# A Mamba-2 scan followed by a hardswish MLP: reordering the opening, and one weight load in four transfers

## The chip, the core and the metric

The kernel runs on one core of one Trainium2 chip. The core has five engines that run side by side, each through its own list of instructions in order: TensorE (PE; weight loads appear as PEld), VectorE (DVE), ScalarE (ACT), GpSimd (POOL) and SyncE (SP), which here only issues DMA transfers. They wait for each other through semaphores. Data come from HBM to the on-chip memory SBUF by DMA; TensorE writes to the eight banks of PSUM. The metric is the device time of one execution in microseconds (us).

## The reference

The first block is a chunked state-space scan over x (4 batches, 8 heads, 768 tokens, 32 channels) with decays a and matrices B and C (16 states). Per chunk it computes

```
cum = cumsum(log(clip(a)))                 # row sums of the logs, per head
L   = exp(cum_i - cum_j), lower triangle
y   = ((C B^T) * L) x  +  (C state) * exp(cum)
state = exp(cum_last) * state + sum_j B_j x_j exp(cum_last - cum_j)
```

The second block takes y as 3072 tokens of 256 features and computes `g = h * clip(h + 3, 0, 6) / 6` with `h = y @ w_in` (256 x 2048), and then `g @ w_out` (2048 x 256). The weights w_in and w_out are float64 in the input.

## The kernel before, in words

The tokens are cut into six chunks of 128 per batch, k = 0 to 5, each with all four batches (512 columns). For a chunk the scan gives yT (features by tokens); then the MLP runs over 16 tiles f of 128 hidden units. For chunk 0 the MLP's first product is `mlp_in` (L647), two full fp32 products for each f; later chunks split the operands (L715). `first_out` (L772) is chunk 0's second product. While the MLP of one chunk runs, the scan of the next is woven into it. The order on every engine is written out by hand in the body of the kernel: what the code calls first stands first in the engine's list, and there is no scheduler.

The float64 weights have to be turned into float32 on the chip. `load_w(i)` starts the DMA of one of eight parts of 1 MB (0 to 3 of w_in, 4 to 7 of w_out) into one of three buffers `raw`, and the generator `decode(i)`, advanced by `weights(i, n)` n steps at a time, does the arithmetic: copy out the top 16 bits (L198, ScalarE), build the significand (L201, L205, VectorE), mask out exponent and sign (L215, L217, VectorE), shift the exponent with two ScalarE activations (L221, L223), join exponent and sign (L228, VectorE) and multiply significand and power into the weight tile (L236, VectorE).

The opening, before the loop over chunks, prepares chunk 0. SyncE issues a, eight transfers of C, x, and the second part of the weights; ScalarE's queue issues the first part and B. The logs of a are summed by `add_up` in two stretches: tokens 0 to 255 first (needed at once for chunks 0 and 1), the other 512 later (L269). The second stretch is stored to DRAM by `store_rows` (L286 `cum_e`, L288 `cum_d`), and later chunks read it back as broadcasts. `turn_cum` (L316) transposes it on TensorE into c_ps, and `by_token` (L319) negates it into cum_n, which biases later chunks' exponentials (L385). For chunk 0, `diff` (L348, L357) makes the differences of sums in PSUM, `diff_exp` (L365) their exponentials L; `ends` (L396, GpSimd) scales B; `turn_b` (L422, L431) transposes B; `turn_squares` (L465) and `part_heads` (L475) transpose C and part it by heads once C has landed; `fade` (L481, GpSimd) scales it; `scores` (L530, and L548 for the state), `multiply` (L564, L574, L579), `mix` (L625, L503) and `keep` (L639) finish yT of chunk 0. `busy(n, bank)` (L493) issues n full-size products of the identity whose result nobody reads.

PSUM banks carry tags: f0 to f3 in one pool, o and y0, y1 in others; a tile with a tag waits until the readers of the tag's last tile are done.

## Time and profile before

| | us |
|---|---|
| median of 3 runs | 340.89 (340.2 to 341.09) |
| the profiled execution | 339.78 |
| its span, first to last instruction | 337.6 |
| TensorE busy | 330.6 (98%) |
| VectorE busy | 234.5 (69%) |
| ScalarE busy | 199.4 (59%) |
| GpSimd busy | 123.9 (37%) |
| first `mlp_in` product (L647) starts | 22.53 |

The profile is of one execution. Durations in it are those of single instructions; a busy share is an average over stages with different limits, and TensorE's busy time is modelled. Each idle time of an engine is put down to what ended it. The chain of waits goes back from the last instruction to whatever released it. L numbers are lines of the kernel before; in the changed kernel the same lines stand three to five further down.

### The profile page before, as it was taken

Reading aid. Unit: us, or ns where it says so; the run is one execution under the profiler, and the core shown is the slowest. Engines: PE = TensorE matmul, PEld = TensorE weight load, DVE = VectorE, ACT = ScalarE, POOL = GpSimd, SP = SyncE. Lnnn points to the kernel's source line nnn. Section 1 sums busy time; section 2 is a strip of 40 time slices with the busy share of each in tenths; the row PEclk is TensorE's granted clock in tenths of the full one; section 3 lists DMA queues with packets and bytes.
Section 4 is the critical chain, followed back from the end, with each engine's and each line's share of the span. In section 5 each row is a group of like instructions: output and inputs, shape, how many; then the busy total and the mean of one; then the engine's idle time right before and its main releaser. Section 6 shows DMA issues by size and latency. Waiting matters only on the chain.

```text
span 337.6 us, 8192 instructions
## 1 busy us (share of the span) xinstructions
PE 330.6 (98%) x3337; PEld 265.4 (79%) x3337; DVE 234.5 (69%) x380; ACT 199.4 (59%) x418; POOL 123.9 (37%) x123
## 2 busy tenths in 40 slices
PE   6999999999999999999999999999999999999996
PEld 2554448888888888888888888888888888899995
DVE  6699999998399739755339556355477355599974
ACT  4769878757986670576461576570486030577661
POOL 3300000290184799089813079911079800000000
PEclk9999999999999999999999999999999999999999
DMA  8999968042590215258107267101160001110001
GB/s 174 165 316 201 208 219 184 2 54 76 139 142 1 57 37 139 33 72 78 33 13 156 33 83 69 28 4 17 27 81 2 2 2 18 26 21 2 1 2 62
DMA packets 89605, 25.15 MB, mean 75 GB/s; under 512 B 82208, under 2 KB 85952, under 8 KB 89056
## 3 DMA queue, kind: packets, MB, share of 16 engines
q1 hardware_dynamic: 85184, 23.33, 37.5%
q10 hardware_dynamic: 4384, 1.31, 1.8%
q8 instruction: 26, 0.43, 0.5%
q14 instruction: 11, 0.09, 0.1%
HBM read 21.33 MB, written 3.29 MB: 73 GB/s over the span
## 4 chain that ended last, share of the span: by engine, by line
PE 94%; DMA 3%; DVE 1%; SPq 1%; issue 0%; DVEq 0%
PE h L715 33%; PE wb L914 13%; PE wc L914 8%; PE o L772 8%; PE h L647 8%; PE wa L914 8%; PE o_end L880 6%; PE y L625 3%; PE y L503 2%; PE cb L530 2%; DMA raw<-in_moe_w_in_dram 2%; DMA pairs<-in_C_dram 1%; PE y L548 1%; SPq L101 1%; PE o_end L898 1%; PE sp L548 0%
## 5 line engine op out<-in xcount | busy, mean ns | idle before, releaser
L759 DVE SCALAR_TENSOR_TENSOR gT<-gT,h 128x512 f32<-128x512 f32 x96 | 64.8, 684 | 33.8 <-ACT gT L754 32.2
L754 ACT ACTIVATE gT<-h,half 128x512 f32<-128x512 f32 x96 | 65.2, 685 | 25.6 <-PE h L715 23.6
L735 ACT ACTIVATE h<-h 128x512 f32<-128x512 f32 x66 | 38.2, 585 | 39.0 <-PE h L715 38.8
L715 PE MATMUL h<-y_hi,w_part 128*128 128x512 f32 x160 | 51.5, 407 | 0.0
L715 PE MATMUL h<-y_less,w_part 128*128 128x512 f32 x160 | 50.1, 399 | 0.0
L715 PE MATMUL h<-y_lo,w_part 128*128 128x512 f32 x160 | 49.5, 395 | 0.0
L818 POOL TENSOR_TENSOR s<-gT 128x512 f32<-128x512 f32 x16 | 23.8, 1490 | 46.7 <-DVE gT L759 46.7
L715 PEld LDWEIGHTS h<-y_lo,w_part 128*128 128x128 f32 x160 | 30.0, 188 | 7.3
L715 PEld LDWEIGHTS h<-y_hi,w_part 128*128 128x128 f32 x160 | 30.0, 188 | 6.8 <-DVE gT L759 0.2
L715 PEld LDWEIGHTS h<-y_less,w_part 128*128 128x128 f32 x160 | 29.2, 188 | 6.0 <-ACT h L735 0.2
L385 ACT ACTIVATE L<-L,cum_n 128x64 f32<-128x64 f32 x128 | 31.6, 336 | 0.0
L772 PE MATMUL o<-w_out,gT 128*128 128x256 f32 x128 | 28.8, 381 | 0.0
L647 PE MATMUL h<-yT,w_in 128*128 128x512 f32 x64 | 27.7, 594 | 0.0
L772 PEld LDWEIGHTS o<-w_out,gT 128*128 128x128 f32 x128 | 24.1, 190 | 3.8 <-issue 0.5
L647 PEld LDWEIGHTS h<-yT,w_in 128*128 128x128 f32 x64 | 12.1, 190 | 14.9 <-issue 13.2
L158 POOL TENSOR_SCALAR_AFFINE_SELECT L<-L 64x1024 f32<-64x1024 f32 (+1 forms) x16 | 20.4, 1281 | 8.5 <-DMA L<-cum_d 8.0
L579 DVE TENSOR_TENSOR L<-L,cb 128x512 f32<-128x512 f32 x24 | 15.0, 681 | 11.7 <-PE cb L530 11.7
L403 POOL TENSOR_TENSOR tmp<-state,eto 128x256 f32<-128x256 f32 x5 | 3.2, 643 | 52.8 <-ACT eto L389 48.9
L818 POOL TENSOR_TENSOR s<-gT,s 128x512 f32<-128x512 f32 x16 | 21.7, 1364 | 0.9
L396 POOL TENSOR_TENSOR bs<-B,L 128x128 f32<-128x128 f32 x24 | 11.2, 486 | 29.5 <-ACT L L385 20.9
L880 PE MATMUL o_end<-v_pair,g_pair 128*128 128x256 f32 x120 | 21.1, 281 | 0.0
L818 POOL TENSOR_TENSOR gT<-gT 128x512 f32<-128x512 f32 x16 | 20.4, 1279 | 0.9
(140 smaller groups left out, 593.0 us busy)
## 6 DMA issues: line engine op xcount, KB each, us to landing
raw<-in_moe_w_out_dram SPq DMA_DIRECT2D x4, 1024.0 KB
L<-cum_d SPq DMA_DIRECT2D x8, 512.0 KB
xt<-in_x_dram SPq DMA_DIRECT2D x6, 512.0 KB
raw<-in_moe_w_in_dram SPq DMA_DIRECT2D x3, 1024.0 KB
out_dram<-back SPq DMA_DIRECT2D x128, 16.0 KB
pairs<-in_C_dram SPq DMA_DIRECT2D x40, 32.0 KB
eto<-cum_e SPq DMA_DIRECT2D x20, 64.0 KB
B<-in_B_dram SPq DMA_DIRECT2D x5, 256.0 KB
```

The costliest lines, as they stand in the source:

```text
L158: nc.gpsimd.affine_select(out=t[rows], in_=t[rows], pattern=pattern, compare_op=ALU.is_ge, fill=-1e5, base=base, channel_multiplier=-1)
L385: nc.scalar.activation(Ls[c][:, b, h], Ls[c][:, b, h], AF.Exp, bias=cum_n[:, c, g:g + 1])
L579: nc.vector.tensor_tensor(out=Ls[c][:, :, hs], in0=Ls[c][:, :, hs], in1=cbs[c][q], op=ALU.mult)
L647: nc.tensor.matmul(out=h, lhsT=w_in[f // FP][:, j, f % FP * P:(f % FP + 1) * P], rhs=yTs[k][:, j].rearrange("p b i -> p (b i)"), start=(j ...
L715: nc.tensor.matmul(out=hs_[k, f], lhsT=w[j][:, f % FP * P:(f % FP + 1) * P], rhs=y[:, j], start=(start and j == 0), stop=True, skip_group_ ...
L735: nc.scalar.activation(h, h, AF.Copy, scale=1.0 / EPS + 1.0)
L754: nc.scalar.activation(gTs[k][:, f], h, AF.Relu, bias=half, scale=1.0 / 6.0)
L759: nc.vector.scalar_tensor_tensor(out=g, in0=g, scalar=1.0, in1=h, op0=ALU.min, op1=ALU.mult)
L772: nc.tensor.matmul(out=o[:, b % 2], lhsT=gTs[0][:, f, b * P:(b + 1) * P], rhs=w_out[:, f], start=(f == 0 and b % 2 == 0), stop=True, skip_ ...
L818: nc.gpsimd.tensor_tensor(out=o, in0=p_, in1=q_, op=op)
L880: nc.tensor.matmul(out=ends_["cross" if n == 2 else "squares"][b], lhsT=g_parts[t][n][:, b * P:(b + 1) * P], rhs=w, start=(t == 0 and b < ...
L914: nc.tensor.matmul(out=bank[:, slot], lhsT=lhs[:, j], rhs=rhs[:, j], start=(clear and j == 0), stop=True, skip_group_check=True)
```

## The change

It has five parts, all in the opening.

- The load of weight part 1 is split by columns into four transfers of 256 KB (rows of 1 KB instead of 4 KB).
- `add_up` of the second stretch is called before `ends(0, b)`, so on VectorE it stands before the transpose of C instead of behind `part_heads`.
- `turn_cum` and `by_token` follow `turn_b`, before the last two `diff`s of chunk 1; c_ps has bank f2 instead of f1, and cum_n is made by ScalarE instead of VectorE. One of the three `busy` products of the stretch, the one behind `turn_cum`, is dropped.
- One step of `decode(0)` (the first ScalarE activation, L221) is called before `turn_b`, so it stands before the copy of B's transpose on ScalarE.
- `decode(0)` has one more step: joining exponent and sign (L228) is now apart from the last product (L236). With the same later calls, it stands before the products of `multiply` (L579) on VectorE, where it had been behind them.

```diff
@@ load_w
-        queue.dma_start(out=dst, in_=src)
+        cuts = range(NP if i == 1 else 1)
+        for c in cuts:
+            sl = slice(c * src.shape[-1] // len(cuts), (c + 1) * src.shape[-1] // len(cuts))
+            queue.dma_start(out=dst[:, :, sl], in_=src[:, :, sl])
@@ decode
         nc.vector.tensor_tensor(out=e, in0=e, in1=s, op=ALU.bitwise_or)
+        if i == 0:
+            yield
         m, e = m.bitcast(FP32), e.bitcast(BF16)
@@ by_token
-        nc.vector.tensor_scalar(
-            out=cum_n[:, 2:], in0=c_ps[:, 2:], scalar1=-1.0, scalar2=None, op0=ALU.mult)
+        nc.scalar.mul(cum_n[:, 2:], c_ps[:, 2:], -1.0)
@@ the opening
     first_eto()
     diff(1, 2, 3)
     weights(0, 1)
+    add_up(ends_at[1])
     for b in range(NB):
         ends(0, b)
+    weights(0, 1)
     turn_b(0)
+    c_ps = ps.tile([P, NC, G], FP32, name="c_ps", tag="f2")
+    turn_cum(c_ps)
+    by_token(c_ps)
     diff(1, 0, 1)
     weights(0, 1)
     diff_exp(1, 2)
     diff_exp(1, 3)
     turn_squares(bcs[0][0], turned(0)[2])
     part_heads(0)
     fade(0, HALF[1], nc.gpsimd)
-    add_up(ends_at[1])
     store_rows()
     load_w(2)
     weights(0, 1)
     busy(2, ps.tile([P, NB * P], FP32, name="d", tag="f3"))
     scores(0)
     multiply(0)
     load_w(3)
-    c_ps = ps.tile([P, NC, G], FP32, name="c_ps", tag="f1")
-    turn_cum(c_ps)
-    busy(1, ps.tile([P, NB * P], FP32, name="d", tag="f0"))
     weights(0, 1)
     weights(1, 1)
-    by_token(c_ps)
     mix(0)
     keep(0)
     weights(1, 3)
```

## The prediction, made before the changed kernel ran

> **What bounds the kernel now.** I read the chain of waits first, because it says which work set the end. TensorE holds 94% of it; the DMA, VectorE and queue pieces all lie in the opening. In order of time, the chain between the last load of C and the first stage of the MLP is:

> ```profile
> 8.91 4.00 DMA pairs<-in_C_dram
> ...
> 13.09 1.17 DVE csT L465
> ...
> 14.28 0.89 DVE cT L475 x2
> ...
> 15.30 1.25 PE cb L530 x59
> ...
> 16.56 1.30 DVE L L579 x2
> ...
> 17.90 0.43 PE c_ps L316 x4
> 18.33 1.05 PE d L493 x2
> 19.39 1.00 PE y L625 x57
> 20.38 0.61 PE y L503 x16
> 20.99 1.00 PE y L625 x54
> 21.99 0.61 PE y L503 x16
> 22.60 27.66 PE h L647 x64
> ```

> Columns: start, length, piece, in us. From 22.5 us on there is nothing but TensorE: 64 matmuls of L647 in 27.66 us are 0.432 us each, without a gap, and the rest of the chain is TensorE until the last VectorE addition at 334.46. So a microsecond saved before the first L647 matmul is saved at the end, as long as TensorE's suppliers keep up. And two pieces of the chain, c_ps (L316) and d (L493, the matmul of `busy`), are not needed by the mix that follows them: they only stand ahead of it on TensorE.

> Second, the timeline of the two engines that feed this stretch, VectorE:

> ```profile
> 13.09 1.16 DVE L465 STREAM_TRANSPOSE csT<-pairs 128x512 f32<-128x512 f32 x1 [2.86 <-DMA pairs<-in_C_dram]
> 15.07 1.21 DVE L269 TENSOR_TENSOR_SCAN pre<-pre 32x512 f32<-32x512 f32 x1
> 16.56 2.48 DVE L579 TENSOR_TENSOR L<-L,cb 128x512 f32<-128x512 f32 x4 [0.28 <-PE cb L530]
> 18.95 0.68 DVE L228 TENSOR_TENSOR we<-we,ws 128x1024 uint16<-128x1024 uint16 x1
> 20.82 0.28 DVE L319 TENSOR_SCALAR cum_n<-c_ps 128x128 f32<-128x128 f32 x1
> ```

> and ScalarE:

> ```profile
> 11.95 0.59 ACT L431 COPY bT<-t_ps 128x512 f32<-128x512 f32 x1 [0.90 <-PE t_ps L422]
> 17.32 0.37 ACT L564 COPY adds<-y 128x256 f32<-128x256 f32 x1 [1.73 <-PE y L548]
> 18.75 1.15 ACT L198 COPY ws<-raw 128x1024 uint16<-128x1024 uint16 x1 [0.53 <-DMA raw<-in_moe_w_in_dram]
> ```

> What to see: VectorE idles 2.86 us before the transpose of C, and ScalarE 0.90 and 1.73 us; these are the holes into which the change moves work. The 0.53 us before L198 says that the second load of weights lands at about 18.75.

> **The change part by part.**

> *Row sums (L269) earlier.* On VectorE the scan goes from behind L475 to behind L217, which ends at 10.23. Its input (L266) has been there since 5.27. It takes 1.21 us, so it ends at 11.5, inside the 2.86 us hole: cost nothing. Without that cover it would cost 1.21.

> *c_ps and cum_n.* The four transposes of L316 go behind those of B (t_ps ends at 11.91; the scan is done by then). They take 0.36 to 0.43 us and push the difference matmuls and the two `busy` matmuls, which ended at 14.88, to 15.24 to 15.31. TensorE had 0.43 us idle before cb at 15.30, waiting for cT, so the delay of cb is 0 to 0.1; I take 0. cum_n becomes a ScalarE copy: no row has it, the nearest are L574 (128x128, 0.31 each of two) and L319 itself (0.28), so 0.3. ScalarE now runs L221 in the hole before bT, then bT (to 12.6), cum_n (to 12.9), L223 and the two exponentials (to about 14.9). The matmuls of the state (L548) that need those start at 16.43, so nothing waits; this stays so up to 1.5 us more. c_ps now sits in a bank that cb needs; cum_n frees it at 12.9, cb comes at 15.3.

> *Signs joined early (L228).* 0.68 us of VectorE go from 18.95 to 15.16, between L475 and the products of L579, where the scan stood before; 1.21 us went in there, so 0.68 do. GpSimd's L481 runs at the same time and had ended at 16.81; were it held up by the whole 0.68, its result at 17.5 would still precede its reader, L503.

> *One `busy` and c_ps leave the chain.* Now the mix (L625) follows the state's matmuls directly. By the built program's list of waits its first matmuls need the first L579 product (17.18) and the copy adds (17.32 + 0.37 = 17.69), and from the fifth on the second product, 17.86. Four matmuls before that are worth about 0.05, so the mix effectively starts at 17.83 instead of 19.31: 1.48 us. The second half of the mix no longer waits for cum_n (in before it paused from 20.92 to 21.15 for it), worth 0 to 0.2. The third and fourth products end at 18.42 and 19.04, before the second half needs them at about 19.4. TensorE alone would reach L647 at 20.85 to 21.05 instead of 22.53.

> *What is late next.* The first L647 needs w_in and the first two copies of yT (L639, 0.37 each). w_in (L236) now follows L579 directly: 18.95 + 1.22 = 20.2, in time. The copies stand behind L198 on ScalarE, which waits for the second load of weights. Landing at L, they end at L + 1.15 + 0.75; at 18.75 that is 20.65, and each microsecond that the load lands after 18.95 now costs one.

> *The load in four transfers.* Rows of 1 KB instead of 4 KB, and three more issues on SyncE, about 0.48 each (the shortest L139), with `cum_e`, `cum_d` and the third and fourth load queued behind them. SyncE waited 2.3 us for the scan at L286 and no longer does, so 3 x 0.48 = 1.4 us more still leaves it earlier: 13.92 + 1.4 = 15.4 instead of 16.31. These stores stay behind the weights in the same queue, so they cannot delay them. Each transfer also waits for the one eight before it: the four pieces for loads of C and B that were in by 11.3, when GpSimd starts on B, and the fourth load now for x, in before the state's matmuls at 16.4. The price of shorter rows: the trace's packets have medians of 159 ns for 4 KB, 84 for 2 KB and 46 for 1 KB (1 KB ones are stores). Each of 16 DMA engines carries 64 packets of 1 KB: 64 x 46 = 2.9 us against 16 x 159 = 2.5, 0.4 later. The other end: a load split by columns could land up to 0.3 earlier, being queued piece by piece. I take 0.3 later, near the packet rows: landing at 19.05, copies done at 20.95.

> [...]

> **The sum.** L647 starts at 21.0 instead of 22.53: 1.5 us. Can the suppliers follow? They are nearly full:

> ```profile
> 22.50:36.00 13.50, 13.50 (x36) 6.05 (x33) 12.62 (x20) 11.37 (x15) 0.00 (x0) 1.00 1.08 214
> 36.00:50.00 14.00, 14.00 (x34) 6.21 (x33) 13.14 (x20) 12.05 (x16) 0.00 (x0) 1.00 0.92 220
> ```

> (windows; after the length TensorE, weight loads, VectorE, ScalarE, GpSimd, granted clock, DMA share, GB/s). VectorE's decoding of the second weights (L215) starts at 20.2 instead of 21.02 and loses the 0.54 it idled at 25.28, so its stream comes 1.3 us earlier, 0.2 behind TensorE's 1.5. The tightest needs are the fourth w_in part (written at 42.33, read by the thirteenth hidden tile at 22.53 + 12 x 1.73 = 43.29) and the first w_out part (49.35 against 50.27): 0.9 us to spare. So all 1.5 us arrive. The profiled execution took 339.78 (span 337.6), 1.1 below the median 340.89; it becomes 338.3, and the median 339.4. A difference of 0.3%, 1.0 us, is about what a measurement of this kernel can tell from none.

> **Rivals.**

> *The clock falls: slower.* Taking out L493 leaves only small-tile matmuls from 15.3 to 21.0, 5.7 us; the longest such stretch in the trace is 3.2 us (19.31 to 22.53), and both have the granted clock at 1.00. If small tiles do not count as activity, it could halve during the mix, at about 19. At the opening matmuls ran from 2.13 and the clock came at about 7.3, so 5.2 us. The mix's remaining 2 us would take 4, and 5.2 us of L647 at half speed lose 2.6: 4.6 lost against 1.5 won, 344.0. It decides from a slow spell of 3 us. Against it: the pause itself shrinks to about 0.4 us, and the clock held through all later mixes. 0.10.

> *The four transfers are paid in line.* If each further one costs 0.63 (the eto loads, 2.51 for four), the load lands 1.9 later still, 20.95, the copies end at 22.85 and L647 starts 0.3 later than before: 341.2. Against it: in the windows 20 to 24 and 24 to 28, where several transfers follow each other, the DMA share stays at 0.97 and 0.86. At 0.53 each nothing is won. 0.07. A far higher price has the last load of C as its bound, 4.00 for 32 KB in the chain: three times that puts L647 at 33, the kernel at 351; 0.05 for prices over 0.9, where it is slower. [...]

> *VectorE absorbs part.* If its stream came no earlier at all, TensorE would use up the 0.9 us of margin and gain only that: 340.0. For it: it is 94% busy; against it: the 0.82 us at L215 follow from two removed rows. 0.12.

> **How the numbers follow.** Forecast 0.66 at 339.4, which is faster by over 0.3%; the two middle rivals, 0.19, are the "same"; 0.15 (the clock, the high price) slower. The range starts at a gain of 1.7 (339.2) less the 0.6 by which runs spread below the median, 338.6, and reaches to 341.3 so that it holds the two middle rivals; it leaves out those two.

> **What would show it.** In the changed profile the chain should go from L579 straight to the mix (now L629), no L321 or L497 between; mix at about 17.8, first h at about 21.0, then 27.66 us without gaps; VectorE's wait for C 1.6 instead of 2.86; L201 of the second weights at about 19.05 and still waiting for its DMA. I am wrong if cb starts after 15.4, if h L651 matmuls take over 0.44 us each, or if L201 starts after 19.5.

## The result, and the profile of the changed kernel

The changed kernel takes 343.32 us (median of 6 runs, 341.81 to 344.27) against 340.51 of the kernel before (6 runs on the same chip, 339.65 to 341.09): a ratio of 1.0078, 95% interval 1.0050 to 1.0107. It is slower, and the range of 338.6 to 341.3 did not hold it. Its profiled execution took 342.29 us, span 340.1, 2.5 more than the one shown of before.

First the chain of waits, the same stretch as in the prediction (start, length, piece, in us):

```profile
15.31 1.20 PE cb L534 x59
...
17.34 0.38 ACT adds L568
...
17.76 0.89 PE y L629 x51
18.65 2.52 issue
21.17 0.31 PE y L629 x6
21.48 0.61 PE y L507 x16
22.09 1.05 PE y L629 x64
23.14 1.04 PE y L507 x9
24.19 28.35 PE h L651 x64
```

Down to the start of the mix (L629) everything stands where it was forecast: cb at 15.31, no c_ps and no `busy` ahead of the mix, and the mix at 17.76 instead of 19.31. Then, inside the mix, a piece that the profile of before did not show: 2.52 us of "issue", time in which the engine waited for nothing that the profile shows. When the mix goes on at 21.17 all that was won is spent. The first h comes at 24.12 by the timeline, 1.59 later than the 22.53 of before, and its 64 matmuls take 28.35 us instead of 27.66.

VectorE (start, length, line, in brackets the idle time before and what ended it) did what it was to do: the scan (L274) lies in the hole before C, the wait for C fell from 2.86 to 1.69, the signs (L231) stand ahead of the products, and w_in (L241) is done at 20.2:

```profile
10.24 1.21 DVE L274 TENSOR_TENSOR_SCAN pre<-pre 32x512 f32<-32x512 f32 x1
13.14 1.11 DVE L469 STREAM_TRANSPOSE csT<-pairs 128x512 f32<-128x512 f32 x1 [1.69 <-DMA pairs<-in_C_dram]
15.08 0.69 DVE L231 TENSOR_TENSOR we<-we,ws 128x1024 uint16<-128x1024 uint16 x1
18.97 1.22 DVE L241 SCALAR_TENSOR_TENSOR w_in<-wm,we 128x1024 f32<-128x1024 f32 x1
```

ScalarE: the new cum_n takes 0.31 and holds up nothing. The second load of weights lets L201 start at 19.80, 1.05 later than in the profile of before, but the copy of yT behind it waits for TensorE, not for L201, which ended at 20.90:

```profile
12.52 0.31 ACT L324 ACTIVATE cum_n<-c_ps 128x128 f32<-128x128 f32 x1
19.80 1.10 ACT L201 COPY ws<-raw 128x1024 uint16<-128x1024 uint16 x1 [1.56 <-DMA raw<-in_moe_w_in_dram]
21.52 0.37 ACT L643 COPY yT<-y 128x256 f32<-128x256 f32 x1 [0.62 <-PE y L629]
```

The windows (after the length: TensorE, weight loads, VectorE, ScalarE, GpSimd, granted clock, DMA share, GB/s) show the second loss:

```profile
18.70:22.12 3.42, 0.95 (x34) 0.79 (x41) 2.64 (x5) 1.47 (x2) 0.00 (x0) 1.00 0.98 334
22.12:25.53 3.41, 3.41 (x82) 2.55 (x82) 2.47 (x5) 2.03 (x4) 0.00 (x0) 0.50 0.84 330
```

After 3.4 us in which TensorE worked for only 0.95, it gets half its clock for the next 3.41 us, and from 25.53 on the full clock again. The first matmul of L776 then starts at 52.37 instead of 50.10, 2.27 later. Of these, 1.59 stand at the first h and 0.68 come behind it. The half clock has a part in both: from the end of the stop to the first h it takes 2.95 us here (21.17 to 24.12) and 2.25 at full clock (20.64 to 22.89 in a second profile of the kernel before, shown below), so 0.70 of the 1.59 are its work, and so are the 0.68. Runs of 341.8 and 342.3 have a mean clock of 0.995 and 0.994, those of 343.2 to 344.3 one of 0.990: by their mean clock, two such stretches come in them, not one.

What does TensorE wait for inside the mix? The page's list of DMA queues names a queue whose packets are instructions:

```profile
q8 instruction: 26, 0.43, 0.5%
```

26 packets in the execution, each of 16,384 bytes by the trace. The page counts 3335 matmuls and 3335 weight loads of TensorE (a matmul is two instructions in the trace, a weight load and a multiplication), about 6,700 instructions: if the packets are TensorE's, some 256 instructions in each, a block. The experiments below have its stops 256 instructions, or a multiple of that, apart. The second of these packets ran from 18.84 to 19.78, in the middle of the stop; in the profile of before it ran from 17.84 to 18.84. In the DMA views of the two stretches, 18.8 to 19.8 of the changed kernel and 17.8 to 18.9 of the kernel before, it is this line:

```profile
q8 instruction: 1, 0.02, 5.8%
...
q8 instruction: 1, 0.02, 5.7%
```

The stop begins behind the 704th of TensorE's traced instructions (recorded waits for a semaphore counted in), which in the changed kernel is the 58th matmul of the mix. That made three theories:

- F, fetch: TensorE has run through its blocks of instructions; the next one comes late because its transfer waits behind data in the DMA queues; the clock falls because TensorE stands still.
- R, the prediction's rival: without the dropped `busy` the clock falls, whatever the block does.
- S, the load: the split load comes late for ScalarE, and that is the loss.

### The profile page after: what moved, and what is told of

Read it like the earlier page. It is cut to its first block, busy times and chain, and to the rows that moved or that the text cites. A ratio compares the mean times of both kernels' runs of the same rounds, so it can differ in the third digit from the quotient of the medians.

```text
span 340.1 us, 8198 instructions
## 1 busy us (share of the span) xinstructions
PE 330.1 (97%) x3335; PEld 265.7 (78%) x3335; DVE 234.4 (69%) x379; ACT 199.6 (59%) x419; POOL 123.6 (36%) x123
## 4 chain that ended last, share of the span: by engine, by line
PE 93%; DVE 3%; ACT 1%; DMA 1%; issue 1%
PE h L719 30%; PE wb L918 12%; PE h L651 8%; PE wc L918 8%; PE o L776 8%; PE wa L918 8%; PE o_end L884 6%; PE y L629 3%; PE y L507 2%; PE cb L534 2%; PE y L552 1%; DMA pre<-in_a_dram 1%; PE d L361 1%; DVE gT L763 1%; DVE w_part L691 1%
## 5 line engine op out<-in xcount | busy, mean ns | idle before, releaser
L776 PE MATMUL o<-w_out,gT 128*128 128x256 f32 x128 | 28.8, 381 | 0.0
L651 PE MATMUL h<-yT,w_in 128*128 128x512 f32 x64 | 28.4, 605 | 0.0
L776 PEld LDWEIGHTS o<-w_out,gT 128*128 128x128 f32 x128 | 24.1, 190 | 3.8 <-issue 0.5
L651 PEld LDWEIGHTS h<-yT,w_in 128*128 128x128 f32 x64 | 12.4, 196 | 15.3 <-issue 13.2
L583 DVE TENSOR_TENSOR L<-L,cb 128x512 f32<-128x512 f32 x24 | 15.0, 682 | 12.8 <-PE cb L534 12.8
L161 POOL TENSOR_SCALAR_AFFINE_SELECT L<-L 64x1024 f32<-64x1024 f32 (+1 forms) x16 | 20.3, 1275 | 8.1 <-PE h L719 5.1
L822 POOL TENSOR_TENSOR s<-gT,s 128x512 f32<-128x512 f32 x16 | 21.3, 1340 | 0.9
L822 POOL TENSOR_TENSOR gT<-gT 128x512 f32<-128x512 f32 x16 | 20.4, 1278 | 0.9
```

The lines of the kernel that those rows point to most:

```text
L161: nc.gpsimd.affine_select(out=t[rows], in_=t[rows], pattern=pattern, compare_op=ALU.is_ge, fill=-1e5, base=base, channel_multiplier=-1)
L583: nc.vector.tensor_tensor(out=Ls[c][:, :, hs], in0=Ls[c][:, :, hs], in1=cbs[c][q], op=ALU.mult)
L651: nc.tensor.matmul(out=h, lhsT=w_in[f // FP][:, j, f % FP * P:(f % FP + 1) * P], rhs=yTs[k][:, j].rearrange("p b i -> p (b i)"), start=(j ...
L776: nc.tensor.matmul(out=o[:, b % 2], lhsT=gTs[0][:, f, b * P:(b + 1) * P], rhs=w_out[:, f], start=(f == 0 and b % 2 == 0), stop=True, skip_ ...
L822: nc.gpsimd.tensor_tensor(out=o, in0=p_, in1=q_, op=op)
```

## The experiments

Each kernel is an edit of the changed kernel or of the kernel before. Times are medians; ratios are against the kernel before in runs on the same chip and go by means, so the two can differ where the runs of a kernel fall into groups. "Block" is the start of the second instruction packet. The stop is given, as the timeline has it, as TensorE's idle time before the rest of the mix. Block, stop and first h are those of one profiled execution; in two executions of the kernel before, the block differs by 0.63 us.

### One transfer again

```diff
-        cuts = range(NP if i == 1 else 1)
+        cuts = range(1)
```

> The changed kernel with the second load of weights in one transfer again. Theory F (TensorE ran out of instructions inside the mix: its next 16 KB block of instructions waits in the DMA queues behind data already queued; the clock then falls because TensorE stood still): the load lands at about 18.75, the instruction packet starts at about 17.8 as in the kernel before instead of 18.8, the mix still stops at its 58th matmul (18.4) but goes on at about 20.1 instead of 21.2, first h matmul at about 22.4; 340.3 if the clock holds, up to 341.5 if the shorter stop still makes it fall. Theory R (the dropped busy product alone lets the clock fall): no better than the changed kernel, 342 to 343.5. Theory S (the late load alone, through ScalarE's copies): no stop, first h at 21.0, 339.0.

Measured: 344.56 us, ratio 1.0109 (1.0065 to 1.0152). The load is in at 19.64, hardly earlier than with four transfers, but the block starts at 20.16, the stop is 3.40 and the half clock lasts 6.8 us. S falls: taking the split back helps nothing. SyncE issued the stores and the third load at 14.7 to 16.2 here, so more data stood in the queues when the block was wanted.

### The split alone, in the kernel before

> The kernel before with only the load split in four. Theory F: the load lands about 1 us later (19.8), the instruction packet starts about 1 us later (18.8), and the first half of the mix, which without it reaches the end of its instructions at 20.05, stops for about 1.1 us until 21.2; first h at about 23.6, 341.6, more if the clock falls. Theory R: busy is still there, the clock holds, 340.5 as before. Theory S: copies of yT end at 21.7, first h still at 22.5, 340.5.

The edit of `load_w` on the kernel before. Measured: 340.94 us, ratio 1.0021 (0.9990 to 1.0052). L201 starts at 20.07, the block at 19.02, and now the kernel before has a stop of 1.17, behind its 704th instruction. Eight of ten executions keep the full clock and lie between 340.4 and 341.4; the two with a lower mean clock took 343.3 and 344.6.

### The `busy` put back

```diff
     load_w(3)
+    busy(1, ps.tile([P, NB * P], FP32, name="d", tag="f0"))
     weights(0, 1)
...
     mix(0)
```

> The changed kernel with the dropped busy product put back between the products of the scores and the mix. Theory F: the mix starts 1.1 us later (18.9) but stops at the same count of instructions (four of them are now the busy product) until the block arrives, about 21.2; first h at about 23.5. TensorE stands still for 1.3 us less, so the clock may hold: 341.5 then, 342.5 if it falls. Theory R: the clock holds and nothing stops, first h at about 22.1, 340.1.

Measured: 344.02 us, ratio 1.0063 (1.0027 to 1.0099). Block 19.56, stop 2.25, and the clock falls for 3.41 us in the profile although the `busy` is there. Two of nine runs kept the full clock, at 340.1 and 340.6. R as the cause falls.

### The load in halves, the second held back

```diff
+            queue.dma_start(out=dst[:, 0], in_=src[:, 0])     # in load_w, for i == 1
...
+    nc.vector.memset(raw.bitcast(FP32)[:, 2 * FP * P:2 * FP * P + 1], 0.0)
+    nc.sync.dma_start(out=dst[:, 1], in_=src[:, 1])
```

> The changed kernel with the second load of weights in two transfers by halves of the rows (4 KB pieces), the second of them held back until VectorE has joined signs and exponents (about 15.8), by a one-column memset into its place. Theory F: the instruction block, which I think is asked for at about 15.9, then stands behind only half of the load: packet starts at 16.0 to 16.8, usable at about 18.5, no stop or a short one in the mix, no fall of the clock; the load lands at about 19.3 and the first h matmul is at 21.3: 339.3. If the block is asked for later than the second half is queued, it is as x1 or the changed kernel, 340.5 to 343. Theory R: the clock falls all the same, 342 to 343. Theory S: the load lands later than 18.95, so 339.5 to 340.

The write into the buffer stands on VectorE behind the joined signs, at about 16.0. Measured: 344.1 us, ratio 1.0103 (1.0072 to 1.0134). The copy of the high halves waits until 21.96, block 18.87, stop 2.36. The block, expected at 16.0 to 16.8, is as late as in the changed kernel, and this run alone does not say why; the later runs use the same means.

### The scan alone, in the kernel before

```diff
     weights(0, 1)
+    add_up(ends_at[1])
...
-    add_up(ends_at[1])
     store_rows()
```

> The kernel before with one edit: the scan L269 stands behind L217 as in the changed kernel, so SyncE no longer waits 2.3 us for it at L286, and the row sums' stores and the third load enter the queues some 2 us earlier. TensorE's and ScalarE's instructions are untouched, the second load is in one transfer. Theory F (TensorE's next 16 KB block of instructions waits in the DMA queues behind the data that was queued before it): the block, fetched at 17.84 to 18.84 before, now starts after the new data, 19.0 to 20.2; TensorE stops at its 705th traced instruction, at about 20.0, for 1.0 to 2.5 us; first h at 23.5 to 25.0; 341.5 to 343 us. Theory R (the dropped busy lets the clock fall) and theory S (the load by columns lands late for ScalarE): nothing that they name is changed, 340.3 to 341.0.

Measured: 343.14 us, ratio 1.0071 (1.0040 to 1.0101), nearly the ratio of the whole change. One VectorE instruction moved into a hole, TensorE and ScalarE untouched. The timeline of TensorE (kernel before with the early scan):

```profile
19.19 0.90 PE L625 MATMUL y<-L,xt 64*32 64x64 f32 x57
21.43 0.31 PE L625 MATMUL y<-L,xt 64*32 64x64 f32 x7 [1.33 <-issue]
```

The block starts at 19.14. This is the run that F alone expected. Four of the ten runs kept the full clock (340.5 to 341.3), six lost part of it (343.0 to 344.9).

### The stores and the third load held back

```diff
+    weights(0, 1)
+    last = cum[:, S - 1:S]
+    nc.vector.tensor_scalar(out=last, in0=last, scalar1=1.0, scalar2=None, op0=ALU.mult)
     store_rows()
     load_w(2)
-    weights(0, 1)
```

> The changed kernel with the second load in one transfer again, and with the row sums' stores and the third load held until VectorE has joined the signs, by a one-element VectorE operation on the row sums (about 16.3 us, as in the kernel before). Theory F with the queue part: the instruction block starts at 17.8 to 18.5 again, not at 20.16 as with one transfer and no hold; the stop at instruction 705 is under 1.8 us instead of 3.6; first h at 22.0 to 23.2; the clock stays at 1.00; 339.8 to 341.2. F without the queue part (the block comes late for a reason of its own): as with one transfer alone, 344.6. R: the busy is still gone, so the clock falls, 343 to 344.5. S: 340.

The changed kernel with one transfer. Measured: 343.24 us, ratio 1.0085 (1.0056 to 1.0113); block 19.07, stop 2.72, clock at half for 10.2 us. Against one transfer without the hold, the block is 1.1 earlier, so what stood behind the load seems to have delayed it; but it is not at 17.8 to 18.5, and the numbers expected of F were wrong. The load itself was still ahead of the block.

### More instructions ahead of the mix

```diff
+    for _ in range(30):
+        nc.tensor.matmul(
+            out=ds[0, 0][:HT, 0], lhsT=ident_h[:, :HT], rhs=hide, start=True, stop=True)
     for b in range(3):
         mask_again(0, b)
```

> The changed kernel with 30 tiny matmuls (64x64, 60 instructions with their weight loads) put into TensorE's hole of 1.5 us at 5.9, ahead of L347; their result is overwritten. Theory F: the block boundary is a matter of the count of instructions, so TensorE now stops after 28 of the mix's first 64 matmuls instead of 58, at about 18.0, and goes on when the block is there, 20.5 to 21.5: a stop of 2.5 to 3.5 us; the clock falls; 343 to 345. R and S: the tiny matmuls lie in a hole and change nothing: the pause stays behind the 58th matmul, 343.3.

Measured: 357.18 us, ratio 1.0474 (1.0431 to 1.0517). The timeline of TensorE in the mix:

```profile
17.84 0.56 PE L629 MATMUL y<-L,xt 64*32 64x64 f32 x28 [0.46 <-ACT adds L568]
21.36 0.63 PE L629 MATMUL y<-L,xt 64*32 64x64 f32 x36 [2.96 <-issue]
...
24.08 0.90 PE L507 MATMUL y<-csT,mid 32*64 32x64 f32 x11
27.83 0.48 PE L507 MATMUL y<-csT,mid 32*64 32x64 f32 x5 [2.85 <-issue]
```

30 matmuls more, and the stop comes exactly 30 matmuls earlier, after 28 instead of 58: again behind instruction 704. A second stop follows behind instruction 960, that is 256 later. The time is far above the 343 to 345 expected, as all later block ends moved too, some of them into the mixes of later chunks. The chain of waits of the same run has, among others, these:

```profile
186.54 1.45 issue
...
237.70 1.82 issue
```

They lie behind instructions 4032 and 5056, which are 704 and multiples of 256, and each is followed by 3.41 us of half clock. Neither R nor S can make a stop that goes by count.

> As the run with 30, with 60 tiny matmuls (120 instructions). Theory F: the block is asked for 120 instructions earlier, at about 13, before the second load of weights is in the queues, and starts before 15.0; the boundary then falls at the end of the state's matmuls, which wait there anyway, so no stop of over 0.6 us in the first half of the mix; the following boundary falls in the last quarter of the mix (about 20.3), where a shorter stop of 0 to 1.5 us may come; first h at 21.5 to 22.8; the clock stays at 1.00; 339.5 to 341.5. R and S: as the changed kernel, 343.3, first h at 24.1.

With 60: 356.31 us (four runs from 349.96 to 359.08, too far apart for a ratio). The stops are again behind 704 (1.87 us, two matmuls before the end of the state's 64 of L552) and behind 960 (2.85). So the place is as F has it, but the block started at 17.63, not before 15.0: it does not start earlier in step with the count, and the time of 339.5 to 341.5 was missed by far.

### The whole load held back

```diff
+            held.append((dst, src, raw))              # in load_w, for i == 1
...
+    dst, src, raw = held[0]                           # behind the joined signs
+    nc.vector.memset(raw.bitcast(FP32)[:, :1], 0.0)
+    nc.sync.dma_start(out=dst, in_=src)
     store_rows()
```

> The changed kernel with the second load in one transfer and held back, by a one-element VectorE write into its buffer behind the joined signs, until about 16.0, that is until TensorE is inside the first cb matmuls and has asked for its next instruction block; the copy of its high halves goes from ScalarE ahead of the mix to VectorE behind the mix's products, so that yT does not wait for the load. TensorE's instructions are those of the changed kernel. Theory F with the queue part: with few data queued ahead of it the block (18.84 in the changed kernel, 20.16 with one transfer) starts at 16.0 to 17.2; no stop of over 0.5 us behind instruction 704; clock 1.00; first h at 21.2 to 22.2; 339.4 to 340.8. F without the queue part: block at 18.5 to 20, stop of 2 to 3.5 us, 342 to 345. R: the busy is still dropped, the clock falls, 343 to 345. S (only the load's landing counts): the load lands at 19.8 to 20.5, but nothing on ScalarE waits for it, 339.4 to 341.

Measured: 343.06 us, ratio 1.0100 (1.0067 to 1.0133). The load's first packet goes at 16.8, the block starts only at 19.51, stop 3.14, half clock for 10.2 us. Missed: no data packet was under way from 15.5 to 16.8 and still the block did not come. Either its request arrives later than that, or it is late for a reason of its own.

> As the kernel with the load held, but the copy of the high halves stays on ScalarE, behind yT instead of ahead of the mix. F with the queue part: block, clock and first h as there (16.0 to 17.2, 1.00, 21.2 to 22.2); VectorE's decoding of the second weights then starts at 22.5 to 23.2 instead of 21, which is 0.6 to 1.3 us beyond what the first h gains, against the 0.9 us of margin: 339.8 to 341.2. F without the queue part, and R: 342 to 345.

The same with the copy left on ScalarE, behind yT: 343.27 us, ratio 1.0090 (1.0055 to 1.0125); block 20.64, stop 4.00. The order of the copies cannot be judged beside such a stop.

### The kernel before without its one `busy`

> The kernel before without the one busy (L493, two matmuls) ahead of the mix, and nothing else. Theory F: the block is fetched when it was before (17.8 to 18.8), the mix starts 0.9 earlier (18.4) but reaches the end of its block at about 19.2 and waits there until 20.2 to 20.4 for instruction 705: first h at 22.4 to 22.8, nothing won: 340.2 to 341.2, the clock at 1.00 if the stop stays under 1.5 us. R: dropping this busy lets the clock fall, 343 to 345. S, and the prediction's own sum: 0.9 us won, 339.6.

Only the line of `busy(1, ...)` is taken out. Measured: 343.06 us, ratio 1.0085 (1.0070 to 1.0101); block 18.70, stop 1.95, and the clock falls for 6.8 us.

By the time alone R had it right and F had not; by the trace it is F's stop, longer than expected, with the clock after it. The `busy` fills time until the block is there: without it TensorE reaches the end of its block 0.9 earlier and stands for it.

### The hold moved further, and a second look at the kernel before

```diff
+            if c == 0 and q == 0:                     # in multiply, behind the first product of L583
+                dst, src, raw = held[0]
+                nc.vector.memset(raw.bitcast(FP32)[:, :1], 0.0)
+                nc.sync.dma_start(out=dst, in_=src)
+                store_rows()
+                load_w(2)
```

> The kernel with the load held (copy on VectorE), with the hold moved from behind the joined signs to behind the first product of L583, about 17.2 instead of 16; the row sums' stores and the third load stay behind it. Queue part of F: the block's request reaches the DMA at about 17.0 and finds nothing there: block at 16.8 to 17.6 (19.51 with the shorter hold), stop behind instruction 704 of 0.3 to 1.5 us instead of 3.35, clock 1.00, first h at 21.4 to 22.6. The load lands at about 21.8, VectorE's decoding of it starts 1.5 later than in the kernel before: 340.2 to 342. Without the queue part (the block late for a reason of its own): block at 18.5 to 20.5, stop of 2 to 4 us, 342.5 to 345.

Measured: 341.61 us, ratio 1.0037 (1.0022 to 1.0052). SyncE issues the load at 17.50, with the shorter hold it was 15.86. The DMA view for the stretches 15.5 to 17.4 and 17.4 to 18.5, one line of each:

```profile
DMA packets 0, 0.00 MB, mean 0 GB/s; under 512 B 0, under 2 KB 0, under 8 KB 0
...
q8 instruction: 1, 0.02, 5.4%
```

and TensorE's timeline:

```profile
17.95 0.90 PE L638 MATMUL y<-L,xt 64*32 64x64 f32 x58 [0.46 <-ACT adds L571]
19.63 0.31 PE L638 MATMUL y<-L,xt 64*32 64x64 f32 x6 [0.77 <-issue]
```

With nothing in its way the block starts at 17.45, the stop is 0.77 instead of 3.14, the clock of the profiled execution stays at 1.00 (as in half of the eight runs, at 340.9 to 341.3), and the first h comes at 21.87, 0.66 earlier than in the first profile of before. The queue part of F holds: the difference to the kernel with the shorter hold is whether the load, with the stores and the third load behind it, is queued by 17 or not. The time does not follow, because the load now lands late: VectorE waits 2.51 us for it, and TensorE then stands 0.87 us for a product of VectorE at 29 and 0.35 for a part of w_in at 44, more than the 0.66 gained.

> As that kernel, but only the second half of the load (by rows k) is held behind the first product; the first half goes out at once and is through at about 17.0. Queue part of F: block at 16.9 to 18.0, stop of 0.3 to 1.7 us, clock 1.00, first h at 21.6 to 22.8; the load is complete at 20.3 to 21: 339.8 to 341.2. Without it: block at 18.5 to 20.5, 342.5 to 345.

Half of the load held: 341.17 us, ratio 1.0026 (1.0006 to 1.0047); block 17.50, stop 1.14. Six of twelve executions keep the clock, at 339.9 to 340.7, six lose part of it, at 341.6 to 343.1.

> The kernel before, unchanged, for a second profile of it. If its first profile was typical, the second load's copy L198 starts at 18.75 (0.3 either way) and the instruction block at 17.84 (0.3 either way). If it was a lucky one, L198 is at 19.4 to 19.9 and the block at 18.5 to 19.1, as in the runs that keep the load in one transfer, with a stop of about 1 us behind instruction 704 and no fall of the clock; the time stays 340.0 to 341.2 either way.

The kernel before: 340.24 us, ratio 0.9995 (0.9984 to 1.0007). L198 starts at 19.09, the block at 18.47, and there is a stop:

```profile
20.64 0.31 PE L625 MATMUL y<-L,xt 64*32 64x64 f32 x7 [0.41 <-issue]
```

So the profile that the prediction was made from showed an execution in which the block was just in time. The kernel before stands at the edge: a stop of 0.41 with the clock kept, and no loss of time that its eight runs (339.79 to 340.99) show.

### The half held, and the `busy` back

> The kernel whose second half of the load is held behind the first product, with the dropped busy put back ahead of the mix (4 more instructions). Theory F: the block starts at 17.4 to 17.7 as there and is usable at about 19.7; TensorE is kept at work by the busy until 18.3 and reaches the end of its block, now two matmuls earlier in the mix, at 19.1 to 19.3: a stop of 0.4 to 0.8 us instead of 1.36, too short to take the clock; clock 1.00 in all runs, first h at 21.8 to 22.4; 339.8 to 340.5, the few tenths below the kernel before that the earlier first h can give. If it is not the stop that takes the clock, some runs show it fallen as there: 341 to 343.

Measured: 341.1 us, ratio 1.0018 (1.0002 to 1.0034). Block 17.93, stop 0.81, and the mean clock is 0.999 or 1.000 in all twelve executions: with the stop short, the clock holds, as expected. The time was missed by 0.6: the first h is at 22.59, and VectorE, which idles 2.42 us for the load, hands over w_in late (TensorE's timeline):

```profile
44.37 7.13 PE L661 MATMUL h<-yT,w_in 128*128 128x512 f32 x16 [0.36 <-DVE w_in L245]
```

Between 25.53 and 45 TensorE works 18.97 of 19.47 us here and 18.25 in the kernel with the whole load held longer, against 19.47 in the kernel before. None of these versions beats the kernel before: in these two, what the earlier block wins is lost again to the late load.

## Why the prediction was wrong, step by step

**Right.** The scan in VectorE's hole, c_ps and cum_n (0.3 forecast, 0.31), cb not delayed, the signs' 0.68 (0.69), the start of the mix (17.83 forecast, 17.76). The part of the sum that moves work between engines was right to 0.1 us.

**The step that failed** is "TensorE alone would reach L647 at 20.85 to 21.05". In its place the profile has a stop of 2.52 us inside the mix, half clock behind it, and the first h at 24.12. The step took TensorE's instructions for given. The mix runs its 64 matmuls, 128 instructions, in 1.1 us, and between the start of cb at 15.3 and the first h lie some 580 instructions, more than two blocks. Each block is a DMA transfer, and the one that begins behind instruction 704 was not there. By these runs it waits behind data: in the three kernels with the later hold it started at 17.45, 17.50 and 17.93, in the first profile of before and with 60 more matmuls at 17.84 and 17.63, in the twelve other profiles at 18.47 to 20.64. Even with the block of before, at 17.84 to 18.84, hardly anything could have been won: in the runs with a stop TensorE went on 1.2 to 1.5 us after the packet's end, which would be 20.0 to 20.3 here, and the rest up to the first h takes 2.25 us at full clock (19.63 to 21.87, 20.64 to 22.89, 21.43 to 23.68): 22.3 to 22.6, against 22.53.

**SyncE's lost wait** was booked as a gain only ("still leaves it earlier"), because the stores stay behind the weights; in the changed kernel they are issued at 15.61 and 16.05, and their first packet of 512 bytes moves at 18.05. They and the third load do not stay behind TensorE's instructions: with both issued earlier, the block started at 19.14 in the kernel before, against 17.84 and 18.47. The early scan alone costs a ratio of 1.0071.

**The load** was sized 0.3 later and landed 1.05 later. The split is likely a part of the reason and not shown to be the whole: alone in the kernel before it landed at 20.07, against 18.75 and 19.09 in two executions of that kernel, but with one transfer and the early scan it also came late, at 19.46, 19.64 and 19.66, each time in one execution. The 18.75 of the profile was an early case, and a sum built on one execution's landing carries at least a third of a microsecond of that. The split alone has a ratio whose interval includes 1. That a load queued piece by piece could land up to 0.3 earlier was the author's estimate; no run shows it. The rival that had the four transfers paid in line put the landing at 20.95; it came at 19.80, and yT did not wait for it.

**The rival of the clock** was priced at 344.0 with a chance of 0.10. The clock did fall and the time is near, but not by its reason, and the moment it named, about 19, was the author's estimate; in the changed kernel half clock began at 22.12. Small tiles did not cost the clock in the profile with the longer hold: it stays at 1.00 from cb at 15.4 to the first h at 21.87. What went with the fall was standing still: with the `busy` back and a stop of 2.25 the clock fell, without it and with 0.77 it held in the profiled execution.

The length of the stop alone does not decide. In the profile of the changed kernel the clock is full for 17.07 us (5.05 to 22.12), half for 3.41 and full again for 314.03 (to 339.56): 5, 1 and 92 times 3.41. In that of before it is full from 7.33 on, no multiple of 3.41 from 5.05. So here the granted clock changes on a grid of 3.41 us, whose place differs from execution to execution, and its falls go with TensorE's work within one window of that grid. Here are the window ahead of the fall with a stop of 1.14 (half of the load held) and the two windows that share the stop of 1.33 (the scan alone), where the clock held; the columns are those of the windows above:

```profile
16.65:20.06 3.41, 1.81 (x123) 1.39 (x102) 3.41 (x6) 0.90 (x3) 0.00 (x0) 1.00 0.54 165
...
17.51:20.92 3.41, 2.32 (x63) 1.36 (x63) 3.38 (x7) 1.73 (x4) 0.00 (x0) 1.00 1.04 393
20.92:24.34 3.42, 2.91 (x105) 2.35 (x106) 3.32 (x8) 1.66 (x5) 0.00 (x0) 1.00 0.97 394
```

From 12 us on, the window just ahead of each of the 15 falls in these profiles had TensorE at work for 0.14 to 2.07 us, and every other window at full clock for 2.31 or more, with one exception of 1.94 (the load in halves). In these profiles a `busy` therefore helps in two ways: it shortens the stop (0.81 with it, 1.14 without, half of the load held), and it fills the 0.46 us that TensorE otherwise waits for `adds` right ahead of the mix, which can lie in the same window, as it does in the first of the three lines. That fits two kernels with nearly the same stop in the profile: without the `busy` (0.77) four of eight runs lost clock, with it (0.81) none of twelve. The windows of runs without a profile are not known, so this last part is argued and not shown.

**VectorE's margin** of 0.9 us was not measured, but its kind was right: in the versions with a short stop, a late load and the clock kept, VectorE's products and w_in are the next things that TensorE waits for.

**The signs named** for being wrong: two of three came. L201 stands at 19.80, after 19.5, and an L651 matmul takes 0.443 us on the mean (28.35 over 64), more than 0.44; cb was in time. None of them would have pointed at the instructions.

What stays open: what fixes the moment of the block's request. With no data under way the block started at 17.45, with little at 17.50, some 1.5 us after the middle of cb, but 120 more instructions ahead of it did not bring it earlier than 17.63, in an execution whose cb came at 16.74. Nor is it shown why the same load lands earlier in some executions than in others, or why half clock lasts one window in some and two or three in others.

## What to carry to other kernels

In this kernel a stretch of tiny matmuls used up instructions faster than they were fetched: the mix's 64 matmuls, 128 instructions, ran in 1.07 us, 256 at that rate in 2.1, while 2.2 to 3.0 us went by from the start of a packet of some 256 to the end of the stop. Count the instructions of such a stretch, and look at when the instruction packets of that engine start and what data is queued ahead of them, before shortening anything in it. Two waits that looked idle were worth their time here: without SyncE's 2.3 us for the scan the ratio is 1.0071, without the `busy` 1.0085. And a stop put down to "issue" that stays at the same count of instructions when work is added ahead of it (704 here, with 30 and with 60 matmuls more) points to the fetch.

## What the runs showed of the hardware

Half clock came in stretches of 3.41, 6.8 and 10.2 us, one, two or three times the same length, and in the opening it began 1.4 to 4.4 us after the stop did (3.47 in the changed kernel, 18.65 to 22.12). It followed windows of 3.41 us with up to 2.07 us of work. Stops of 1.17 and 1.33 us left the clock at 1.00 in the profiled execution, one of 1.14 did not; the two windows of the stop of 1.33 have 2.32 and 2.91 us of work, the one of 1.14 has 1.81.
